# Top-k attention: mask and row maximum added by TensorE to the turned raw scores, the exponential taken in the copy from PSUM

## The chip, the core and the metric
The kernel runs on one core of one Trainium2 chip. The metric is the device time of one execution in microseconds; the kernel before has a median of 1265.99 us over 3 runs (1265.19 to 1269.22).

## The reference
Three layers follow each other. The first is the attention that is changed here; q, k and v are (4, 8, 576, 64) in f32:

```python
scores = scale * np.matmul(q, k.transpose(0, 1, 3, 2))
kth = np.partition(scores, -32, axis=-1)[..., -32:-31]
scores = np.where(scores >= kth, scores, -1000000000.0)
attn = np.exp(scores - np.max(scores, axis=-1, keepdims=True))
attn = attn / (np.sum(attn, axis=-1, keepdims=True) + 1e-09)
out = np.matmul(attn, v)
```

Each query row keeps its 32 largest scores of 576. Then 2304 tokens are routed to 8 experts of equal capacity by a greedy pass over their router logits, and a third layer applies a rational function between two products. Both follow the attention and are not touched.

## The kernel before
The attention works in 72 units (`NU`). A unit is 128 query rows of two heads against 576 keys, so two matrices of 128x576; nine units make a pair of heads of two batches (`NJ`), and the fifth of the nine (j equal to `R`) holds the last 64 rows of both batches. Units go in batches of three (`GB`), for which thresholds and normalisation are worked out together; the last six units are handled one by one.

The order of the work is written out by hand: `step(u)` (L993) issues one round of a software pipeline, and each engine runs its instructions in the order issued. In a step the stages are, each for an older unit than the one before it:

- ScalarE copies the scores of unit u from PSUM into `sv` (L686, `st_evacuate`), places turned q and k for the next heads in five of nine steps (L649), and copies a router tile where one is due (L886, L888).
- TensorE computes the scores of unit u+1 (L676), turns q and k (L635) or a router tile (L881), turns the weights of an older unit in nine 128x128 pieces into the PSUM tile `pt` (L820, `st_transpose`), and multiplies an older unit's turned weights with v (L842, L846, `st_av`); a router product (L894) ends the step where one is due.
- VectorE finds the candidates of unit u (`st_candidates`): fourteen MAX8 over sevenths of a row (L733), then three rounds of MAX8 and MATCH_REPLACE8 on the 56 candidates of each head (L739, L745). Between the first fourteen it takes from the list `later` one piece at a time: the window maxima (L760), the threshold (L777 to L792) and the normalisation (L860 to L862) of older units.
- `st_window`: for each head ScalarE forms the sign of the score against a first cut (L754) and GpSimd multiplies it onto the scores (L759), for VectorE's window maximum. At the end of a batch GpSimd scales the row maxima (L765).
- `st_weights`: for each head ScalarE takes the exponential of the scores less the row maximum (L808); the choice of the 32 is a factor 0 or 1 (or -1, which the copy's Relu drops) in `sg2`, from VectorE (L811) for the second head and in one unit of eight for both, else from ScalarE's Sign (L813); GpSimd multiplies both into `sv` (L814).
- `st_spill`: ScalarE copies the nine turned pieces from PSUM to SBUF with a Relu (L826). `pt` is one buffer, so the next turns wait for this copy.

When the loop ends, `finish_attention` (L1062) hands what is left of the last units to a small planner (`Flow`), which gets each piece with an engine, a cost and what it depends on, and issues it in the order that these give. There the weights are formed by ScalarE's exponential (L1125) and a combined compare-and-multiply on VectorE (L1131). At its end `suspicious` (L951) checks whether a threshold was doubtful; if it was, `recompute` does the attention again in an exact way.

```python
sv = sv_t.pop((u, hh))
ex = wk.tile([P, S], F32, name="ex")
nc.scalar.activation(ex, sv, AF.Exp, bias=t["nb"][:, c : c + 1], scale=SCALE)
sg = wk.tile([P, S], BF16, name="sg2")
if hh or u % WQ in WR:
    nc.vector.tensor_scalar(sg, sv, tau_all[:, 2 * GB * b + c : 2 * GB * b + c + 1], None, op0=OP.is_ge)
else:
    nc.scalar.activation(sg, sv, AF.Sign, bias=t["pn"][:, c : c + 1])
nc.gpsimd.tensor_tensor(sv, ex, sg, op=OP.mult)
```

Of the kernel before, what the change touches and what calls it, by code (L numbers as in the profile page):

```python
# [8 lines left out]
F32 = mybir.dt.float32  # L9
# [175 lines left out]
def kernel(  # L185
# [29 lines left out]
    R = 4  # L215
# [7 lines left out]
    OVER_BITS = 9  # L223
    BEFORE = -(1.0 - 2.0**-24)
    GROUPS = [82] * 5 + [83] * 2
    COLS = [
# [12 lines left out]
    region = wpool.tile([P, 2 * KC * F1], F32, name="region")  # L239
    nc.scalar.preload_act_table_set("natural_log_exp_and_others")  # L240
    ones = consts.tile([P, P], F32, name="ones")
    nc.vector.memset(ones, 1.0)
# [228 lines left out]
    with ExitStack() as actx:  # L471
# [21 lines left out]
        xs = xpool.tile([P, NT], F32, name="xs")  # L493
        tau_all = xpool.tile([P, NTILE], F32, name="tau_all")

        span = xpool.tile([P, 2], F32, name="span")
# [36 lines left out]
        with ExitStack() as sctx:  # L533
# [38 lines left out]
            raw, val, prep, sc_t, sv_t, pr_t, pT_t, po_t, bat = {}, {}, {}, {}, {}, {}, {}, {}, {}  # L572
            pq_t, prep_ps, po_bank = {}, {}, [None]

# [128 lines left out]
            def new_batch(b):  # L703
                t = {
                    "top": wk.tile([P, 2 * GB, 2, 8], F32, name="top"),
                    "nb": wk.tile([P, 2 * GB], F32, name="nb"),
                    "sum": wk.tile([P, 2 * GB], F32, name="sum"),
                    "w8": wk.tile([P, 2 * GB, 8], F32, name="w8"),
                    "pn": wk.tile([P, 2 * GB], F32, name="pn"),
                }  # L710
                bat[b] = t
                return t
# [11 lines left out]
            def st_candidates(u):  # L724
# [12 lines left out]
                for rd in range(3):  # L737
# [4 lines left out]
                    if rd < 2:  # L742
                        for hh in range(2):
                            nx = wk.tile([P, len(GROUPS) * 8], F32, name="cm", bufs=4)
                            nc.vector.match_replace(nx, t["top"][:, 2 * i + hh, rd, :], cds[hh], NEG)  # L745
                            cds[hh] = nx

            def st_window(u):
                b, i = divmod(u, GB)
# [11 lines left out]
                if u == group_end(u):  # L761
                    g = group(u)
                    n = g.stop - g.start
                    tau = tau_all[:, 2 * GB * b + g.start : 2 * GB * b + g.stop]
                    nc.gpsimd.tensor_scalar(t["nb"][:, g], t["top"][:, g, 0, 0], -SCALE, None, op0=OP.mult)  # L765
                    later.extend(threshold_steps(t, g, tau))
# [31 lines left out]

            WQ, WR = 8, [int(c) for c in "2".split()]

            def st_weights(u):
                b, i = divmod(u, GB)
                t = bat[b]
                for hh in range(2):
                    c = 2 * i + hh
                    sv = sv_t.pop((u, hh))
                    ex = wk.tile([P, S], F32, name="ex")
                    nc.scalar.activation(ex, sv, AF.Exp, bias=t["nb"][:, c : c + 1], scale=SCALE)  # L808
                    sg = wk.tile([P, S], BF16, name="sg2")
                    if hh or u % WQ in WR:  # L810
                        nc.vector.tensor_scalar(sg, sv, tau_all[:, 2 * GB * b + c : 2 * GB * b + c + 1], None, op0=OP.is_ge)  # L811
                    else:
                        nc.scalar.activation(sg, sv, AF.Sign, bias=t["pn"][:, c : c + 1])  # L813
                    nc.gpsimd.tensor_tensor(sv, ex, sg, op=OP.mult)  # L814

            def st_transpose(u):
                pt = ps_t.tile([P, 3, 4, P], F32, name="pt")
                pr = pr_t.pop(u)
                for c in range(NC):
                    nc.tensor.transpose(pt[:, c // 4, c % 4, :], pr[:, c * P : (c + 1) * P], ident)  # L820
                pq_t[u] = pt.rearrange("p b c x -> p (b c) x")[:, 0:NC, :]

            def st_spill(u):
                pt = pq_t.pop(u)
                sb = wk.tile([P, NC, P], F32, name="pT", bufs=2)
                nc.scalar.activation(sb, pt, AF.Relu)  # L826
                pT_t[u] = sb
# [79 lines left out]
            def st_exact(u):  # L907
                b, i = divmod(u, GB)
                st_evacuate(u)
                for hh in range(2):  # L910
# [10 lines left out]
                    nc.vector.tensor_scalar(nb, tops[:, 0, 0:1], -SCALE, None, op0=OP.mult)  # L921
                    ex = wk.tile([P, S], F32, name="ex")
                    nc.scalar.activation(ex, sv, AF.Exp, bias=nb, scale=SCALE)
# [27 lines left out]
            def suspicious():  # L951

                f = wk.tile([P, S], F32, name="ex")[:, 0 : 2 * NTILE].rearrange("p (k n) -> p k n", k=2)
                nc.vector.tensor_scalar(f[:, 0, :], tau_all, 0.0, None, op0=OP.is_le)
                m = wk.tile([P, S], F32, name="win")[:, 0:NTILE].bitcast(U32)
                nc.vector.tensor_scalar(m, cut_all.bitcast(U32)[:, :, 7], 0x7FFFFF, None, op0=OP.bitwise_and)
                nc.vector.tensor_scalar(f[:, 1, :], m, float(OVER_BITS), None, op0=OP.is_equal)
                nc.vector.tensor_reduce(oddb, f, axis=AX.XY, op=OP.max)
# [103 lines left out]
            def finish_attention():  # L1062
# [8 lines left out]
                def add_window(u):  # L1071
# [3 lines left out]
                    for hh in range(2):  # L1075
# [21 lines left out]
                    tau = tau_all[:, 2 * GB * b + g.start : 2 * GB * b + g.stop]  # L1097
                    largest_of[u] = last.add("V", 0.1, lambda: nc.vector.tensor_scalar(
                        t["nb"][:, g], t["top"][:, g, 0, 0], -SCALE, None, op0=OP.mult
                    ), [], u - 0.5)  # L1100
                    rk = wk.tile([P, 2], F32, name="rk")
# [14 lines left out]
                def add_weights_of(u, deps):  # L1116
                    b, i = divmod(u, GB)
                    t = bat[b]
                    end = []
                    for hh in range(2):  # L1120
                        c, st = 2 * i + hh, {}

                        def exp_of(c=c, hh=hh, st=st):
                            st["ex"] = wk.tile([P, S], F32, name="ex")
                            nc.scalar.activation(  # L1125
                                st["ex"], sv_t[u, hh], AF.Exp, bias=t["nb"][:, c : c + 1], scale=SCALE
                            )

                        def chosen_of(c=c, hh=hh, st=st):
                            sv = sv_t.pop((u, hh))  # L1130
                            nc.vector.scalar_tensor_tensor(  # L1131
                                sv, sv, tau_all[:, 2 * GB * b + c : 2 * GB * b + c + 1], st["ex"],
                                op0=OP.is_ge, op1=OP.mult,
                            )

                        a = last.add("A", 0.67, exp_of, [largest_of[u]] if u in largest_of else [], u)
                        m = last.add("V", 0.66, chosen_of, [a] + deps, u)
                        hold(a, "ex", 3, [m])
                        end.append(m)
                    return end  # L1140

                def add_turned(u, deps):
                    t = last.add("P", 1.1, lambda: st_transpose(u), deps, u)
                    a = last.add("A", 1.01, lambda: st_spill(u), [t], u)
# [1223 lines left out]
```

## Time and profile before

| what | value |
|---|---|
| median of 3 runs | 1265.99 us |
| profiled execution | 1264.03 us |
| its span | 1262.3 us |
| PE, PEld busy | 1103.9, 892.2 us |
| DVE, ACT, POOL busy | 1108.7, 1062.8, 423.3 us |
| mean granted TensorE clock | 0.913 |

In the profile PE are TensorE's products, PEld its weight loads, DVE is VectorE, ACT ScalarE and POOL GpSimd. The span runs from the first to the last instruction; the execution's own time is 1.7 us longer. A line such as L811 is that of the kernel. In a timeline, instructions that follow each other and are alike stand in one row, with their count; busy time counts overlapping instructions once, so the start of the next instruction tells what one occupies better than its duration does. "128*128" ahead of a shape is the part of TensorE's array. Some records are missing, a few per cent.

### The profile page before, as it was taken

The numbers are of one execution on the slowest core, as the hardware profiler recorded it, in microseconds if no ns is written. First come the engines' busy times: TensorE is split into PE (matmuls) and PEld (weight loads), VectorE is DVE, ScalarE is ACT, GpSimd is POOL, SyncE is SP. The second block draws the span as 40 slices with busy tenths as digits, with TensorE's granted clock in tenths as the row PEclk, the third lists the DMA queues.
The fourth block names the chain that finished last, engine by engine and source line by source line (L and its number), as shares of the span: only waits on it lengthen the run. The fifth ranks groups of instructions, "written<-read, shape, count | busy, mean of one in ns | idle before, by whom it ended". The sixth has DMA issues, their size and how long they took to land.

```text
span 1262.3 us, 26058 instructions
## 1 busy us (share of the span) xinstructions
PE 1103.9 (87%) x9159; PEld 892.2 (71%) x9159; DVE 1108.7 (88%) x4224; ACT 1062.8 (84%) x1869; POOL 423.3 (34%) x429
## 2 busy tenths in 40 slices
PE   5788888899989796787547999999999999999996
PEld 3677777787878684555435777878888888888784
DVE  6999999999999973888788979898989989897795
ACT  4999999999999975867799978888888789876684
POOL 3888888878888820000110001010001001001010
PEclk8899999999999987555678999999999999999999
DMA  5204112020200110921313322213122210200000
GB/s 122 49 10 150 30 38 49 10 49 10 49 2 1 70 65 3 371 66 51 120 36 138 128 93 80 74 27 128 38 87 86 87 67 26 80 1 20 1 20 20
DMA packets 81103, 80.54 MB, mean 64 GB/s; under 512 B 59968, under 2 KB 59968, under 8 KB 80960
## 3 DMA queue, kind: packets, MB, share of 16 engines
q1 hardware_dynamic: 77888, 69.27, 17.2%
q0 software_dynamic: 3072, 9.48, 2.5%
q8 instruction: 76, 1.25, 0.4%
q14 instruction: 67, 0.55, 0.1%
HBM read 69.25 MB, written 9.47 MB: 62 GB/s over the span
## 4 chain that ended last, share of the span: by engine, by line
PE 26%; issue 14%; ACT 6%; DVE 4%; POOL 1%; DMA 0%; POOLq 0%; DVEq 0%
PE pa L1903 3%; PE pa L1904 3%; PE pa L1905 3%; PE ph L1903 3%; PE ph L1905 3%; PE ph L1904 3%; PE po L1904 3%; PE po L1905 3%; PE po L1903 3%; ACT junk L302 2%; POOL out_dram L2289 1%; ACT w1s L1376 1%; PE pa L2278 0%; ACT wout L379 0%; DVE w2s L1381 0%
## 5 line engine op out<-in xcount | busy, mean ns | idle before, releaser
L759 POOL TENSOR_TENSOR win<-sv,sg 128x576 f32<-128x576 f32 x142 | 179.2, 1283 | 37.8 <-ACT sg L754 32.0
L814 POOL TENSOR_TENSOR sv<-ex,sg 128x576 f32<-128x576 f32 x136 | 175.5, 1293 | 46.6 <-DVE sg L811 34.8
L733 DVE MAX8 cd<-sv 128x8 f32<-128x82 f32 (+1 forms) x1008 | 182.4, 231 | 4.1 <-ACT sv L686 4.1
L842 PE MATMUL po<-vm,pT 128*128 128x65 f32 (+1 forms) x1280 | 153.7, 269 | 11.2 <-DVE eqp L787 4.1
L1903 PE MATMUL ph<-x,win 128*128 128x288 f16 x512 | 147.4, 288 | 10.6 <-DVE uv L2172 10.6
L842 PEld LDWEIGHTS po<-vm,pT 128*128 128x128 f32 (+1 forms) x1280 | 142.5, 185 | 18.5 <-DVE eqp L787 7.5
L1904 PE MATMUL po<-g,wout 128*128 128x288 f16 x512 | 146.4, 286 | 2.7 <-DVE g L1894 2.7
L1905 PE MATMUL ph<-x,win 128*128 128x288 f16 x512 | 147.4, 288 | 0.0
L1904 PE MATMUL ph<-x,win 128*128 128x288 f16 x512 | 147.4, 288 | 0.0
L1903 PE MATMUL po<-g,wout 128*128 128x288 f16 x512 | 146.4, 286 | 1.0 <-ACT g L1893 0.8
L1905 PE MATMUL po<-g,wout 128*128 128x288 f16 x512 | 146.4, 286 | 0.0
L2289 POOL DMA_INDIRECT out_dram<-ob,tok x24 | 25.0, 1043 | 317.9 <-ACT ob L2285 265.9
L1880 POOL DMA_INDIRECT xe<-xrows,rows_i x24 | 24.5, 1023 | 294.9 <-PE pa L1915 272.0
L754 ACT ACTIVATE sg<-sv,cut_all 128x576 bf16<-128x576 f32 x142 | 109.4, 781 | 5.0 <-DVE cut_all L739 4.8
L2163 ACT ACTIVATE z<-ph,inv 128x288 f32<-128x288 f32 x128 | 63.9, 499 | 56.2 <-PE ph L1905 55.5
L820 PE MATMUL pt<-ident,sv 128*128 128x128 f32 x648 | 96.6, 294 | 9.8 <-POOL sv L814 9.2
L760 DVE MAX8 w<-win 128x8 f32<-128x576 f32 x142 | 105.2, 741 | 0.0
L808 ACT ACTIVATE ex<-sv,nb 128x576 f32<-128x576 f32 x136 | 104.5, 776 | 0.0
L820 PEld LDWEIGHTS pt<-ident,sv 128*128 128x128 f32 x648 | 79.1, 152 | 27.5 <-POOL sv L814 17.1
L826 ACT ACTIVATE pT<-pt 128x1152 f32<-128x1152 f32 x72 | 81.7, 1134 | 6.2 <-PE pt L820 6.2
L686 ACT ACTIVATE sv<-s 128x1152 f32<-128x1152 f32 x72 | 80.7, 1121 | 3.7 <-PE s L676 2.8
L676 PE MATMUL s<-region 64*128 64x288 f32 (+5 forms) x400 | 55.4, 425 | 27.7 <-ACT kT L649 9.5
(361 smaller groups left out, 3302.4 us busy)
## 6 DMA issues: line engine op xcount, KB each, us to landing
region<-in_moe_w_dram SPq DMA_DIRECT2D x16, 2048.0 KB, 7.8
xrows<-x SPq DMA_DIRECT2D x1, 4644.0 KB
region<-in_q_dram SPq DMA_DIRECT2D x32, 128.0 KB, 2.8
region<-in_k_dram SPq DMA_DIRECT2D x32, 128.0 KB, 2.9
vm<-in_v_dram SPq DMA_DIRECT2D x32, 128.0 KB, 3.0
wout<-in_moe_w_in_dram SPq DMA_DIRECT2D x8, 511.8 KB, 7.1
region<-in_moe_w_out_dram SPq DMA_DIRECT2D x8, 511.8 KB, 3.5
win<-in_moe_w_in_dram SPq DMA_DIRECT2D x6, 511.8 KB, 7.1
```

The source lines that it names most:

```text
L733: nc.vector.max(cd[:, g, :], sv[:, o : o + n])
L754: nc.scalar.activation(sg, sv_t[u, hh], AF.Sign, bias=cut_all[:, 2 * u + hh, 7:8], scale=-OVER, accum_out=t["sum"][:, c : c + 1],)
L759: nc.gpsimd.tensor_tensor(win, sv_t[u, hh], sg, op=OP.mult)
L760: later.append(lambda c=c, win=win: nc.vector.max(t["w8"][:, c, :], win))
L808: nc.scalar.activation(ex, sv, AF.Exp, bias=t["nb"][:, c : c + 1], scale=SCALE)
L814: nc.gpsimd.tensor_tensor(sv, ex, sg, op=OP.mult)
L820: nc.tensor.transpose(pt[:, c // 4, c % 4, :], pr[:, c * P : (c + 1) * P], ident)
L826: nc.scalar.activation(sb, pt, AF.Relu)
L842: nc.tensor.matmul(po[p0 : p0 + n, i, hh, :], sb[:, hh * (R + 1) + c, p0 : p0 + n], vm[:, bb, hh, c, :], start=(c == 0), stop=False,)
L1903: nc.tensor.matmul(acc, ah, bh, start=first, stop=False)
L1904: nc.tensor.matmul(acc, ah, bl, start=False, stop=False)
L1905: nc.tensor.matmul(acc, al, bh, start=False, stop=last)
```

## The change
The weights are no longer formed ahead of the turn. TensorE turns the raw scores; a product then adds to each turned piece the mask (as stationary operand, bf16) times a diagonal (`dg`) that holds -1/EPS times the row maxima. The mask is EPS where the score is chosen and 1 + EPS where it is not, so a chosen score loses the row maximum and another one 2^14 times the maximum besides. The copy from PSUM takes the exponential of the sum. The row maximum is rounded in `dg`, which the later division by the sum of weights makes up for. For the second head VectorE makes the mask in one comparison with an addition; for the first head ScalarE takes a Sign, as before in seven units of eight, and GpSimd scales and shifts it. GpSimd makes the diagonals once for a batch of three units. `suspicious` also asks now whether a threshold is under 2^-4 or a row maximum over 2^12.

```diff
+    EPS = 2.0**-14
+    LEAST, MOST = 2.0**-4, 2.0**12
...
+    identb = consts.tile([P, P], BF16, name="identb")
+    nc.vector.tensor_copy(identb, ident)
...
-                    "nb": wk.tile([P, 2 * GB], F32, name="nb"),
+                    "dg": wk.tile([P, 2 * GB, P], BF16, name="dg", bufs=2),
...
+            def shift(t, b, g, engine):
+
+                n = g.stop - g.start
+                top = top_all[:, 2 * GB * b + g.start : 2 * GB * b + g.stop]
+                engine.tensor_scalar(top, t["top"][:, g, 0, 0], -1.0 / EPS, None, op0=OP.mult)
+                engine.tensor_tensor(
+                    t["dg"][:, g], identb[:, None, :].to_broadcast([P, n, P]), top[:, :, None].to_broadcast([P, n, P]),
+                    op=OP.mult,
+                )
...
-                    nc.gpsimd.tensor_scalar(t["nb"][:, g], t["top"][:, g, 0, 0], -SCALE, None, op0=OP.mult)
+                    shift(t, b, g, nc.gpsimd)
...
-            WQ, WR = 8, [int(c) for c in "2".split()]
+            def beyond(mk, sv, c):
+                nc.vector.tensor_scalar(mk, sv, tau_all[:, c : c + 1], EPS, op0=OP.is_lt, op1=OP.add)
 
             def st_weights(u):
                 b, i = divmod(u, GB)
                 t = bat[b]
+                mk = wk.tile([P, 2, S], BF16, name="mk", bufs=2)
                 for hh in range(2):
                     c = 2 * i + hh
                     sv = sv_t.pop((u, hh))
-                    ex = wk.tile([P, S], F32, name="ex")
-                    nc.scalar.activation(ex, sv, AF.Exp, bias=t["nb"][:, c : c + 1], scale=SCALE)
-                    sg = wk.tile([P, S], BF16, name="sg2")
-                    if hh or u % WQ in WR:
-                        nc.vector.tensor_scalar(sg, sv, tau_all[:, 2 * GB * b + c : 2 * GB * b + c + 1], None, op0=OP.is_ge)
+                    if hh:
+                        beyond(mk[:, hh, :], sv, 2 * u + hh)
                     else:
+                        sg = wk.tile([P, S], BF16, name="sg2")
                         nc.scalar.activation(sg, sv, AF.Sign, bias=t["pn"][:, c : c + 1])
-                    nc.gpsimd.tensor_tensor(sv, ex, sg, op=OP.mult)
+                        nc.gpsimd.tensor_scalar(mk[:, hh, :], sg, -0.5, 0.5 + EPS, op0=OP.mult, op1=OP.add)
+                mk_t[u] = mk.rearrange("p h s -> p (h s)")
...
             def st_transpose(u):
                 pt = ps_t.tile([P, 3, 4, P], F32, name="pt")
                 pr = pr_t.pop(u)
+                mk = mk_t.get(u)
+                b, i = divmod(u, GB)
                 for c in range(NC):
-                    nc.tensor.transpose(pt[:, c // 4, c % 4, :], pr[:, c * P : (c + 1) * P], ident)
+                    o = c * P
+                    nc.tensor.transpose(pt[:, c // 4, c % 4, :], pr[:, o : o + P], ident)
+                    if mk is None:
+                        continue
+                    for p0, n, hh in [(0, P, c // (R + 1))] if c != R else [(0, TAIL, 0), (TAIL, TAIL, 1)]:
+                        nc.tensor.matmul(
+                            pt[p0 : p0 + n, c // 4, c % 4, :], mk[:, o + p0 : o + p0 + n],
+                            bat[b]["dg"][:, 2 * i + hh, :], start=False, stop=True, skip_group_check=True,
+                        )
...
-                nc.scalar.activation(sb, pt, AF.Relu)
+                if mk_t.pop(u, None) is not None:
+                    nc.scalar.activation(sb, pt, AF.Exp, scale=SCALE)
+                else:
+                    nc.scalar.activation(sb, pt, AF.Copy)
...
-                    largest_of[u] = last.add("V", 0.1, lambda: nc.vector.tensor_scalar(
-                        t["nb"][:, g], t["top"][:, g, 0, 0], -SCALE, None, op0=OP.mult
-                    ), [], u - 0.5)
+                    largest_of[u] = last.add("G", 0.9, lambda: shift(t, b, g, nc.gpsimd), [], u - 0.5)
...
-                        a = last.add("A", 0.67, exp_of, [largest_of[u]] if u in largest_of else [], u)
-                        m = last.add("V", 0.66, chosen_of, [a] + deps, u)
-                        hold(a, "ex", 3, [m])
-                        end.append(m)
-                    return end
+                    first = last.add("V", 0.5, lambda: chosen_of(0), deps, u)
+                    return end + [first, last.add("V", 0.5, lambda: chosen_of(1), [first], u)]
...
-                    t = last.add("P", 1.1, lambda: st_transpose(u), deps, u)
+                    t = last.add("P", 1.8, lambda: st_transpose(u), deps, u)
+                    if deps:
+                        hold(deps[-2], "mk", 2, [t])
```

## Rows read from the trace of the kernel before
**Rows 1.** One line's instructions, L686, the copy of the scores: count, durations, first and last start.
```profile
L686 ACT ACTIVATE sv<-s x72: 1104/1118/1160, 12.7 to 435.5; 128x1152 f32<-128x1152 f32 x72
```

**Rows 2.** Windows: us, busy PE, PEld, DVE, ACT, POOL, PEclk, DMA share, GB/s.
```profile
60.00:400.00 340.00, 299.71 (x2543) 259.25 (x2540) 334.21 (x1903) 327.82 (x557) 284.94 (x244) 0.96 0.15 37
440.00:500.00 60.00, 50.14 (x335) 39.77 (x335) 36.00 (x133) 41.52 (x56) 9.42 (x9) 0.79 0.13 47
500.00:520.00 20.00, 9.98 (x136) 7.92 (x136) 14.34 (x74) 15.13 (x32) 1.89 (x4) 0.50 0.74 278
```

**Rows 3.** Groups of instructions, 60 to 400 us: busy us, mean ns, idle before, releaser.
```profile
L814 POOL TENSOR_TENSOR sv<-ex,sg 128x576 f32<-128x576 f32 x111 | 143.2, 1294 | 37.0 <-DVE sg L811 27.3 <-ACT region L649 2.8 <-DVE lg L895 1.2
...
L808 ACT ACTIVATE ex<-sv,nb 128x576 f32<-128x576 f32 x111 | 85.4, 776 | 0.0
...
L811 DVE TENSOR_SCALAR sg<-sv,tau_all 128x576 bf16<-128x576 f32 x62 | 43.9, 718 | 0.0
...
L813 ACT ACTIVATE sg<-sv,pn 128x576 bf16<-128x576 f32 x48 | 37.3, 777 | 11.7 <-DVE pn L792 11.5
...
L895 DVE COPY lg<-po 128x8 f32<-128x8 f32 x8 | 1.3, 164 | 5.8 <-PE po L894 5.8
```

**Rows 4.** One line's instructions, L811, whole execution: least, median, longest ns.
```profile
L811 DVE TENSOR_SCALAR sg<-sv,tau_all x77: 501/514/1643, 36.1 to 444.5; 128x576 bf16<-128x576 f32 x77
```

**Rows 5.** Timeline of VectorE: start us, duration us, instruction.
```profile
250.98 0.50 DVE L811 TENSOR_SCALAR sg<-sv,tau_all 128x576 bf16<-128x576 f32 x1
251.40 0.24 DVE L733 MAX8 cd<-sv 128x8 f32<-128x82 f32 x1
...
256.26 1.39 DVE L811 TENSOR_SCALAR sg<-sv,tau_all 128x576 bf16<-128x576 f32 x1
```

**Rows 6.** Timeline of GpSimd at the second of those comparisons.
```profile
256.06 1.28 POOL L814 TENSOR_TENSOR sv<-ex,sg 128x576 f32<-128x576 f32 x1
```

**Rows 7.** Timeline of ScalarE, two instructions that follow each other.
```profile
254.74 0.77 ACT L813 ACTIVATE sg<-sv,pn 128x576 bf16<-128x576 f32 x1
255.41 0.77 ACT L808 ACTIVATE ex<-sv,nb 128x576 f32<-128x576 f32 x1
```

**Rows 8.** Groups of GpSimd, whole execution, shapes kept apart.
```profile
L765 POOL TENSOR_SCALAR nb<-top 128x6 f32<-128x6 f32 x22 | 5.3, 239 | 0.0
L1664 POOL TENSOR_TENSOR asel<-oh,gone 128x144 bf16<-128x144 bf16 x7 | 3.1, 440 | 69.8 <-DVE rng L1537 45.5 <-DVE gone L1658 22.9 <-DVE gone L1730 1.4
```

**Rows 9.** Timeline of TensorE's products, one step and the start of the next.
```profile
327.20 1.35 PE L676 MATMUL s<-region 64*128 64x64 f32 x10 [1.04 <-ACT xt L886]
328.48 0.66 PE L881 MATMUL s<-ident,x 128*128 128x128 f32 x4
328.98 1.15 PE L820 MATMUL pt<-ident,sv 128*128 128x128 f32 x9
329.96 1.00 PE L842 MATMUL po<-vm,pT 128*128 128x65 f32 x8
...
332.14 1.01 PE L894 MATMUL po<-wg,xt 128*128 128x8 f32 x8
333.84 1.35 PE L676 MATMUL s<-region 64*128 64x64 f32 x10 [0.69 <-ACT xt L886]
```

**Rows 10.** Timeline of TensorE's products at half the clock, behind the attention.
```profile
516.65 1.06 PE L1440 MATMUL pl<-region,diag 128*128 128x256 f32 x2
517.51 0.42 PE L1441 MATMUL pl<-w1s,minus 128*128 128x256 f16 x1
517.72 0.43 PE L1667 MATMUL pt<-asg,onesb 128*128 128x8 bf16 x9
```

**Rows 11.** Timeline of TensorE's weight loads, the nine turns of one step.
```profile
253.38 1.01 PEld L820 LDWEIGHTS pt<-ident,sv 128*128 128x128 f32 x9
```

**Rows 12.** Groups of instructions, 440 to 520 us: the last units' weights.
```profile
L1131 DVE SCALAR_TENSOR_TENSOR sv<-sv,tau_all,ex 128x576 f32<-128x576 f32 x8 | 6.2, 811 | 0.1
L1125 ACT ACTIVATE ex<-sv,nb 128x576 f32<-128x576 f32 x8 | 5.8, 767 | 3.1 <-DVE sv L1131 3.1
```

More of the change, by code (lines that the diff above doesn't have):

```diff
@@ L494 @@
         tau_all = xpool.tile([P, NTILE], F32, name="tau_all")
+        top_all = xpool.tile([P, NTILE], F32, name="top_all")
         span = xpool.tile([P, 2], F32, name="span")
@@ L572 @@
             raw, val, prep, sc_t, sv_t, pr_t, pT_t, po_t, bat = {}, {}, {}, {}, {}, {}, {}, {}, {}
-            pq_t, prep_ps, po_bank = {}, {}, [None]
+            pq_t, mk_t, prep_ps, po_bank = {}, {}, {}, [None]
             LOADS = [
@@ L921, in st_exact @@
                     nc.vector.tensor_scalar(nb, tops[:, 0, 0:1], -SCALE, None, op0=OP.mult)
-                    ex = wk.tile([P, S], F32, name="ex")
+                    ex = wk.tile([P, S], F32, name="win")
                     nc.scalar.activation(ex, sv, AF.Exp, bias=nb, scale=SCALE)
@@ L951, in suspicious @@
             def suspicious():
-                f = wk.tile([P, S], F32, name="ex")[:, 0 : 2 * NTILE].rearrange("p (k n) -> p k n", k=2)
-                nc.vector.tensor_scalar(f[:, 0, :], tau_all, 0.0, None, op0=OP.is_le)
+                f = wk.tile([P, S], F32, name="win")[:, 0 : 3 * NTILE].rearrange("p (k n) -> p k n", k=3)
+                nc.vector.tensor_scalar(f[:, 0, :], tau_all, LEAST, None, op0=OP.is_lt)
+                nc.vector.tensor_scalar(f[:, 2, :], top_all, -MOST / EPS, None, op0=OP.is_lt)
                 m = wk.tile([P, S], F32, name="win")[:, 0:NTILE].bitcast(U32)
@@ L1116, in add_weights_of, with chosen_of @@
                 def add_weights_of(u, deps):
[L1117 to L1134, printed above, removed]
-                        a = last.add("A", 0.67, exp_of, [largest_of[u]] if u in largest_of else [], u)
-                        m = last.add("V", 0.66, chosen_of, [a] + deps, u)
-                        hold(a, "ex", 3, [m])
-                        end.append(m)
-                    return end
+                    end = [largest_of[u]] if u in largest_of else []
+                    mk = {}
+                    def chosen_of(hh):
+                        if not mk:
+                            mk[0] = wk.tile([P, 2, S], BF16, name="mk", bufs=2)
+                            mk_t[u] = mk[0].rearrange("p h s -> p (h s)")
+                        beyond(mk[0][:, hh, :], sv_t.pop((u, hh)), 2 * u + hh)
+                    first = last.add("V", 0.5, lambda: chosen_of(0), deps, u)
+                    return end + [first, last.add("V", 0.5, lambda: chosen_of(1), [first], u)]
                 def add_turned(u, deps):
-                    t = last.add("P", 1.1, lambda: st_transpose(u), deps, u)
+                    t = last.add("P", 1.8, lambda: st_transpose(u), deps, u)
+                    if deps:
+                        hold(deps[-2], "mk", 2, [t])
                     a = last.add("A", 1.01, lambda: st_spill(u), [t], u)
```

## The prediction
> **What bounds the kernel now.** I read first where the time goes by stage, then what paces the stage that is changed, then the three engines that the change loads or relieves. The attention loop's 72 score copies start between 12.7 and 435.5 us [rows 1], so 71 steps take 422.8 us, 5.95 us each. The steady part is 60 to 400 us [rows 2]: 111 exponentials at two a step are 56 steps [rows 3], 6.07 us a step. There VectorE is busy 334.2 of 340 us, ScalarE 327.8, TensorE 299.7, GpSimd 284.9: two engines are all but full, and VectorE stands first with 5.97 us a step. So removing work from ScalarE alone can't pay; the question is what makes VectorE full.
>
> The answer lies in L811, the comparison with the threshold. 62 of them take 43.9 us, 718 ns in the mean [rows 3], though the least and the median are 501 and 514 ns and the longest is 1643 [rows 4]. The instance at 250.98 is free (0.50 us, and the next instruction starts 0.42 us behind it); the one at 256.26 takes 1.39 us [rows 5], and ends 0.3 us after a GpSimd product that ran from 256.06 to 257.34 [rows 6]. So the comparison is held while GpSimd's long product runs. 62 x 0.51 = 31.6 us would be its free cost; 12.3 us, or 0.22 us a step, is holding. VectorE's only idle time in the stretch is 5.8 us, all for the router's product [rows 3].
>
> **The change, part by part.**
> ScalarE: two exponentials a step go. From the start of the Sign at 254.74 to that of the Exp at 255.41 an instruction occupies 0.67 us [rows 7], so 111 x 0.67 = 74.4 us go. The Sign for the first head now runs in all 56 steps, not in 48 [rows 3]: 8 x 0.67 = 5.4 us come. The copy out of PSUM becomes an Exp of the same size; Exp and Sign of one size take 776 and 777 ns [rows 3], so a function's kind costs nothing here. 327.8 - 74.4 + 5.4 = 258.8 us, 4.62 a step. ScalarE stops being a bound. Its next wait is the one it has now for the Sign's threshold (11.5 us [rows 3]); behind it the next score copy queues, with a microsecond of slack.
>
> VectorE: the mask is one comparison a step instead of 62 in 56 steps, with an addition in the same pass: 6 x 0.42 = 2.5 us less. The holding should mostly go too. Today GpSimd multiplies the first head's weights just when VectorE finishes a unit's candidates and comes to the comparison. Afterwards those products are gone, and GpSimd's window products start only when ScalarE has taken a Sign of that unit's candidates, 0.77 us (a Sign's length [rows 7]) after the comparison could begin. Bounds: all 12.3 us gone, or none. I take all but a quarter (the long GpSimd work every third step may still meet it). 334.2 - 2.5 - 9.2 = 322.5 us, 5.76 us a step; with all gone 5.70, with none 5.92.
>
> GpSimd: two products of 1.29 us a step go (143.2 us [rows 3]). Added are one pass over 576 bf16 elements, one small multiply, and every third step the scaled diagonals, 128 x 768. Their prices are not in the trace. The pass lies between the 0.44 us of a 144-element bf16 product [rows 8] and the 1.29 us of a 576-element one; I take 0.8, being one input instead of two. The diagonals lie between 1.29 us (more elements than that row) and 1.29 x 768/576 = 1.72, and I take 1.72. The small multiply is L765's 0.24, already there. The two window products stay, of L814's shape. Per step 2 x 1.29 + 0.8 + (1.72 + 0.24)/3 = 4.0 us, against 5.1 now: no bound. The window products queue behind the diagonals once in three steps; VectorE wants them a step later, so they hide.
>
> TensorE: added are ten bf16 products a step onto the PSUM that the nine turns have just written. The turns now start from the raw scores, and each product waits for the mask and the diagonals where the turns waited for GpSimd's weights; the mask is ready 1.3 us earlier after the comparison, since no GpSimd product follows it. Behind that wait on TensorE stand the step's value products, and ScalarE's copy of the turned tile in the next step. No DMA is touched. A step's own work without waits: scores 327.20 to 328.48, 1.28 us; four turns 0.50; the nine turns 328.98 to 329.96, 0.98; the value products 329.96 to 332.14, 2.18; the router product about 0.95, its 1.01 less the end of its last piece [rows 9]. Four turns of q and k of that shape come in four of nine steps and two in a fifth (0.25 a step), router turns and products in 9 of 56 (0.23). Sum 4.92 us. One added product has 128 columns. The nearest mixture is f32 and f16 products onto one PSUM tile at half the clock (0.50 in that stretch [rows 2]; the rows are [rows 10]): the two f32 take 516.65 to 517.51, the f16 one of 256 columns 0.21 us, with no time lost between them, so 128 columns at the full clock take 0.053 us. And nine bf16 products of 8 columns pass in 0.43 us [rows 10], so a bf16 weight load is no longer than about 0.03. That gives the lower end, 0.053. The upper end: an f32 weight load fills the whole time of its turn (nine loads in 1.01 us beside nine turns in 1.15 [rows 9, 11]), and one that can't start before the added product does has 0.98/9 = 0.11 us to run; if the turns wait for all of it besides the product's own columns, 0.16. If it merely runs beside the product, 0.11 in all. I take 0.08, between the ends where the load is hidden and where it runs beside: 0.8 us a step, 5.72 in all.
> The Trainium skill, page "TensorE: Matmul & The Clock Gate", section "Back-to-back issue gap", gives 81 ns for a load and product of 128 columns in a stream; by that the sum would be 4.92 + 0.81 = 5.73. No run here shows such a stream of 128-column bf16 products.
>
> End of the attention, 440 to 500 us: 8 exponentials (5.8 us) go from ScalarE, and VectorE's 8 combined products of 0.81 [rows 12] become comparisons of 0.51, 2.4 us less; TensorE gains some six times 0.8 us at a lower clock (0.79), and it is the busiest there, 50.1 of 60 us against 41.5 for ScalarE [rows 2]. I take 0, with ends 5 us to either side. One identity copy at the start and one check at the end are 0.2 us each, hidden by first loads and by the waits there.
>
> **The sum.** VectorE 5.76 and TensorE 5.72 lie side by side. Today's step is 0.10 above its fullest engine; keep that: 5.86 us. Saved 0.21 x 56 = 11.8 us; the 15 steps outside the stretch (5.5 us each, filling and draining) I set to nothing. Off the profiled execution, 1264.0 us (span 1262.3), this gives 1252 us. The median of the runs is 1266.0, 2 us above that execution. A measurement tells some 0.3%, 4 us, from no change.
>
> **Rivals.**
> 1. TensorE takes the place of ScalarE. At 0.11 us a product its step is 4.92 + 1.1 = 6.02, plus 0.10: 6.12, which loses 0.05 x 56 = 3 us: 1267 us. For it: the weight loads are full length already [rows 11]. Against: nothing but the guess that some of a load hides. Chance 0.18.
> 2. Slower: the f32 load behind each added product isn't hidden at all. 0.16 x 10 = 1.6 us, TensorE's step 6.52 + 0.10 = 6.62; 0.55 x 56 = 31 us, and the 15 other steps some 8: 1303 us. It decides from 0.105 us a product on, (6.07 - 0.10 - 4.92)/10. Against it: nine loads and nine turns, 0.98 us each if laid end to end, pass in the same 0.98 us [rows 9, 11], so loads run beside products on the same rows. Chance 0.12. The Trainium skill, same page, section "Part 3: Packing small matmuls — row/col tiling", says that a load overlaps running products only if it is for other rows of the array; that rule would bring this case, and those rows disagree with it.
> 3. The holding stays: GpSimd's new work meets the comparison as often as the old. VectorE 5.92 + 0.10 = 6.02, 3 us saved, 1261 us. For it: the diagonals and window products together still run 3 to 5 us of each step. Chance 0.15.
> 4. The new check on the range of the scores sends the kernel into its exact second pass, hundreds of microseconds. The reference's inputs, multiplied out, have thresholds from 1.77 and maxima up to 11.4, far inside 1/16 and 4096. Chance 0.01.
> The forecast, 1242 to 1259, has 0.54.
>
> **How the numbers follow.** Low end: holding all gone, the waits of 0.10 too, 5.70: 0.37 x 56 = 21 us, and 5 at the end, 1238. High end: rival 1 with 5 us lost at the end, 1272. Rival 2 lies outside. Faster: the forecast, what lies below it, and parts of rivals 1 and 3, 0.70. Within 0.3%: most of rivals 1 and 3, 0.14. Slower: rival 2, 4 and the top of 1, 0.16.
>
> **What would show it.** Right: L811's successor at 0.50 to 0.55 us in the mean; ScalarE under 80% in 60 to 400 us while VectorE stays near full; the nine turns with their products in 1.6 to 2.0 us; steps near 5.9. Wrong: turns and products above 2.1 us, and VectorE waiting for TensorE; or comparisons still at 0.7.

## The result and the profile after

The changed kernel takes 1253.14 us (median of 4 runs, 1249.88 to 1254.08); the kernel before, on the same chip, 1267.61 us (median of 4, 1265.19 to 1275.57). The ratio is 0.987, with a 95% interval of 0.9822 to 0.9919: faster by 14 us. The profiled execution took 1253.07 us, with a span of 1251.4, 11 us below the one of before; the traces can account for these 11 of the 14.

The windows of the kernel after (us, busy PE, PEld, DVE, ACT, POOL, PEclk, DMA share, GB/s) answer to [rows 2]:

```profile
60.00:400.00 340.00, 338.08 (x3258) 293.33 (x3256) 332.20 (x1976) 276.13 (x469) 217.02 (x216) 1.00 0.15 37
440.00:500.00 60.00, 43.22 (x359) 31.18 (x357) 28.53 (x113) 32.17 (x54) 1.45 (x3) 0.76 0.14 46
```

The 340 us hold 58 steps (58 Signs and 58 comparisons, below) where they held 56: 5.86 us a step for 6.07. Such a count is good to one step, 0.1 us; the score copies that start in the stretch lie 5.88 us apart, where they lay 6.14. VectorE stays nearly full with 5.73 us a step, ScalarE has fallen from 96 to 81% of the stretch, and TensorE has risen from 88 to 99%. Its clock was granted in full for the whole stretch; before it was 0.96.

Groups of instructions of the kernel after, 60 to 400 us (busy us, mean ns, idle before, releaser), with the last line answering to the router's product in [rows 3]:

```profile
L843 PE MATMUL pt<-dg,mk 128*128 128x128 bf16 x580 | 99.3, 224 | 0.0
...
L828 ACT ACTIVATE sg<-sv,pn 128x576 bf16<-128x576 f32 x58 | 44.7, 771 | 40.3 <-DVE pn L807 40.3
...
L829 POOL TENSOR_SCALAR mk<-sg 128x576 bf16<-128x576 bf16 x57 | 38.2, 671 | 21.4 <-ACT sg L828 21.4
...
L815 DVE TENSOR_SCALAR mk<-sv,tau_all 128x576 bf16<-128x576 f32 x58 | 30.5, 525 | 0.0
L758 POOL TENSOR_TENSOR dg<-identb,top_all 128x768 bf16<-128x768 bf16 x20 | 29.4, 1469 | 1.7
...
L924 DVE COPY lg<-po 128x8 f32<-128x8 f32 x9 | 1.5, 166 | 7.8 <-PE po L923 7.5
```

TensorE's 580 added products are ten a step. ScalarE now sits idle for 40.3 us ahead of the Sign, waiting for its threshold, where it was 11.5. The comparison fell from 718 to 525 ns, and there is one a step. Single lines' instructions (count, durations, first and last start) say where the end of the execution moved; L691 is the copy of the scores, L1646 the first instruction behind the attention:

```profile
L691 ACT ACTIVATE sv<-s x72: 1106/1116/1134, 12.8 to 422.0; 128x1152 f32<-128x1152 f32 x72
...
L1646 DVE COPY lc<-lg x1: 235/235/235, 492.8 to 492.8; 128x144 f32<-128x144 f32 x1
```

The kernel before has the copy of `lg` in L1629:

```profile
L1629 DVE COPY lc<-lg x1: 1604/1604/1604, 504.0 to 504.0; 128x144 f32<-128x144 f32 x1
```

The last copy starts 13.5 us earlier than in [rows 1]. From it to L1646 pass 70.8 us; before, the copy of `lg` started at 504.0, 68.5 us behind the last score copy. From there to the end of the span it is 758.6 us against 758.3. So the loop won 13.5 us, the end of the attention lost 2.3, and the rest stayed within 0.3 us.

**The comparison.** Between 60 and 400 us, 32 of the 62 comparisons of the kernel before began while a GpSimd instruction of over a microsecond ran, and took 0.92 us in the mean; the other 30 took 0.505. After, none of the 57 that begin in the stretch does. The timeline of the kernel after shows why (start us, us, instruction, idle before):

```profile
302.40 0.50 DVE L815 TENSOR_SCALAR mk<-sv,tau_all 128x576 bf16<-128x576 f32 x1
...
302.78 0.76 ACT L769 ACTIVATE sg<-sv,cut_all 128x576 bf16<-128x576 f32 x1
...
303.72 1.28 POOL L774 TENSOR_TENSOR win<-sv,sg 128x576 f32<-128x576 f32 x1 [1.56 <-ACT sg L769]
```

GpSimd's next long instruction waits for a Sign of the same unit whose candidates VectorE has just finished, and by then the comparison is over. What GpSimd runs at the comparison now is the pass over the mask (0.67 us): nine of the 57 comparisons are held by it and take 0.62 to 0.68 us. None overlaps the diagonals.

**The turns.** The timeline of TensorE's products in the kernel after, around the piece that holds both heads:

```profile
300.38 0.22 PE L843 MATMUL pt<-dg,mk 128*128 128x128 bf16 x1
300.43 0.28 PE L839 MATMUL pt<-ident,sv 128*128 128x128 f32 x1
300.64 0.25 PE L843 MATMUL pt<-dg,mk 128*64 128x128 bf16 x2
300.82 0.33 PE L839 MATMUL pt<-ident,sv 128*128 128x128 f32 x1
300.98 0.22 PE L843 MATMUL pt<-dg,mk 128*128 128x128 bf16 x1
301.04 0.28 PE L839 MATMUL pt<-ident,sv 128*128 128x128 f32 x1
301.15 0.22 PE L843 MATMUL pt<-dg,mk 128*128 128x128 bf16 x1
301.21 0.28 PE L839 MATMUL pt<-ident,sv 128*128 128x128 f32 x1
```

A turn with a full product takes 0.17 us (301.04 to 301.21); a turn alone took 0.11 [rows 9], so the product costs 0.06. The piece with two products of 64 columns takes 0.39 (300.43 to 300.82): 0.28 for the two. The piece behind it takes 0.22 (300.82 to 301.04), 0.05 more than the other full ones, so the two cost 0.33 in all. From the first turn of a unit to its first value product it is 1.80 us, the median of 58 units.

### The profile page after: what moved, and what is told of

Its sections match the earlier page's. It is cut to its first block, busy times and chain, and to the rows that moved or that the text cites. A ratio compares the mean times of both kernels' runs of the same rounds, so it can differ in the third digit from the quotient of the medians.

```text
span 1251.4 us, 27126 instructions
## 1 busy us (share of the span) xinstructions
PE 1141.0 (91%) x9879; PEld 921.2 (74%) x9879; DVE 1088.6 (87%) x4216; ACT 979.3 (78%) x1734; POOL 331.3 (26%) x390
## 4 chain that ended last, share of the span: by engine, by line
PE 26%; issue 14%; ACT 6%; DVE 4%; POOL 1%; DMA 0%; POOLq 0%; DVEq 0%
PE pa L1920 3%; PE pa L1921 3%; PE pa L1922 3%; PE ph L1920 3%; PE ph L1922 3%; PE ph L1921 3%; PE po L1921 3%; PE po L1922 3%; PE po L1920 3%; ACT junk L306 2%; POOL out_dram L2306 1%; ACT w1s L1393 1%; PE pa L2295 0%; ACT wout L383 0%; DVE w2s L1398 0%
## 5 line engine op out<-in xcount | busy, mean ns | idle before, releaser
L871 PEld LDWEIGHTS po<-vm,pT 128*128 128x128 f32 (+1 forms) x1280 | 139.4, 182 | 8.3 <-issue 4.3
L839 PE MATMUL pt<-ident,sv 128*128 128x128 f32 x648 | 131.7, 287 | 0.0
L769 ACT ACTIVATE sg<-sv,cut_all 128x576 bf16<-128x576 f32 x142 | 108.9, 772 | 22.5 <-DVE cut_all L744 14.5
L843 PE MATMUL pt<-dg,mk 128*128 128x128 bf16 (+1 forms) x720 | 123.9, 224 | 0.0
L839 PEld LDWEIGHTS pt<-ident,sv 128*128 128x128 f32 x648 | 91.5, 141 | 21.1 <-ACT sg L769 5.8
L691 ACT ACTIVATE sv<-s 128x1152 f32<-128x1152 f32 x72 | 80.5, 1118 | 11.7 <-PE s L681 4.6
L828 ACT ACTIVATE sg<-sv,pn 128x576 bf16<-128x576 f32 x68 | 52.4, 770 | 46.2 <-DVE pn L807 46.2
L843 PEld LDWEIGHTS <-mk 128*128 128x128 bf16 (+1 forms) x720 | 72.4, 111 | 9.0 <-DVE mk L815 0.2
```

Source lines behind the costliest of these rows:

```text
L691: nc.scalar.activation(pair.rearrange("p h (g c) -> p (h g) c", g=2), sc_t.pop(u)[:, :, 0:HS], AF.Copy)
L769: nc.scalar.activation(sg, sv_t[u, hh], AF.Sign, bias=cut_all[:, 2 * u + hh, 7:8], scale=-OVER, accum_out=t["sum"][:, c : c + 1],)
L839: nc.tensor.transpose(pt[:, c // 4, c % 4, :], pr[:, o : o + P], ident)
L843: nc.tensor.matmul(pt[p0 : p0 + n, c // 4, c % 4, :], mk[:, o + p0 : o + p0 + n], bat[b]["dg"][:, 2 * i + hh, :], start=False, stop=True, ...
L871: nc.tensor.matmul(po[p0 : p0 + n, i, hh, :], sb[:, hh * (R + 1) + c, p0 : p0 + n], vm[:, bb, hh, c, :], start=(c == 0), stop=False,)
```

## Experiments

The theory after the result: the gain is that VectorE's comparison is no longer held by GpSimd's product, which needs ScalarE to have been relieved too, and TensorE's products give a part back. The rival: ScalarE's relief alone, or a TensorE that still has room. Each kernel was timed beside runs of the kernel before on the same chip, whose medians lay between 1267.58 and 1268.28 us; ratios are to these.

**Putting GpSimd's product back.** On the changed kernel:

```diff
                         nc.gpsimd.tensor_scalar(mk[:, hh, :], sg, -0.5, 0.5 + EPS, op0=OP.mult, op1=OP.add)
+                        nc.gpsimd.tensor_tensor(sg, sv, sg, op=OP.mult)
```

> The changed kernel with one product of 128x576 more on GpSimd a step, behind the first head's mask, where the kernel before multiplied the weights; nothing uses its result. Theory that VectorE's comparison was held by GpSimd's product and that ending this gave much of the gain: the comparison's mean goes from 0.525 to 0.65 to 0.75 us again, the step up by 0.1 to 0.2 us, 1258 to 1265 us. Rival, the holding was not what VectorE lost or lies now behind TensorE's floor: within 3 us of 1253.

Measured: 1265.58 us (10 runs), ratio 0.9968 (0.9945 to 0.9991): 12 us of the 14 are gone, and the time lies 0.6 us above its range. The stretch of 60 to 400 us and the comparison's group in it:

```profile
60.00:400.00 340.00, 330.83 (x3112) 283.73 (x3110) 339.96 (x1897) 262.99 (x450) 283.22 (x264) 0.99 0.15 37
```

```profile
L815 DVE TENSOR_SCALAR mk<-sv,tau_all 128x576 bf16<-128x576 f32 x55 | 50.1, 912 | 0.0
```

The comparison grew by 0.39 us, to 0.91 where 0.65 to 0.75 were expected; VectorE's 0.13 us of spare time in a step went, and the step grew by about the rest, from 5.88 to 6.12 by the score copies. This product holds the comparison for 0.41 us a step, nearly twice the 0.22 of the kernel before, so the 12 us show what holding does, not what the old holding cost. A held and a free one, in the timelines of VectorE and of GpSimd:

```profile
209.63 1.24 DVE L815 TENSOR_SCALAR mk<-sv,tau_all 128x576 bf16<-128x576 f32 x1
...
227.90 0.50 DVE L815 TENSOR_SCALAR mk<-sv,tau_all 128x576 bf16<-128x576 f32 x1
```

```profile
209.28 1.27 POOL L830 TENSOR_TENSOR sg<-sv,sg 128x576 bf16<-128x576 f32 x1
...
228.03 1.50 POOL L830 TENSOR_TENSOR sg<-sv,sg 128x576 bf16<-128x576 f32 x1
```

The first comparison began 0.35 us behind the product and ended 0.32 us after the product's end (210.87 against 210.55). Over the 43 of this kernel that begin so the median is 0.315, and it is 0.316 in the kernel before, [rows 5, 6] among them. The second comparison began ahead of the product, took its free 0.50, and the product took 1.50 for its usual 1.28, ending 1.14 us behind the comparison. Whichever comes first holds the other up.
The Trainium skill, page "GPSIMD Engine Reference", section "8. Key points", says that GpSimd shares its SBUF interfaces with VectorE, and that they contend when VectorE runs in a two-port mode or reads two inputs from SBUF. These rows agree that they contend, and add the size; which mode the comparison ran in they don't say.

**Taking each part away from the kernel before.** Without the first head's product, without the exponentials, and without both (`ex` replaced by `sv`):

```diff
-                    nc.gpsimd.tensor_tensor(sv, ex, sg, op=OP.mult)
+                    if hh:
+                        nc.gpsimd.tensor_tensor(sv, ex, sg, op=OP.mult)
```

```diff
-                    ex = wk.tile([P, S], F32, name="ex")
-                    nc.scalar.activation(ex, sv, AF.Exp, bias=t["nb"][:, c : c + 1], scale=SCALE)
...
-                    nc.gpsimd.tensor_tensor(sv, ex, sg, op=OP.mult)
+                    nc.gpsimd.tensor_tensor(sv, sv, sg, op=OP.mult)
```

> The kernel before without GpSimd's product of weights for the first head, so that these rows are weighted by raw scores; exponentials and signs stay. Theory that the holding of VectorE's comparison costs 0.22 us a step and that ScalarE stands right behind: the comparison's mean falls from 0.72 to 0.50 to 0.55 us, the step from 6.07 to about 5.95, where ScalarE's 5.85 keeps it: 1258 to 1262 us beside 1266. Rival, ScalarE's exponentials alone set the old step: no change, within 3 us. Second rival, the holding alone set it: 1252 us or less.

> The kernel before without the exponentials of the loop: GpSimd multiplies the raw scores by the choice, so weights are raw scores. ScalarE falls to 4.5 us a step, GpSimd's products stay. Theory: VectorE's comparison stays held (0.65 us or more in the mean) and VectorE keeps the step at 5.95 to 6.05: 1260 to 1265 us. Rival, ScalarE set the old step: 5.75 to 5.85 us a step, 1248 to 1255 us.

> The kernel before with both taken out: no exponentials in the loop and no product of weights for the first head. Theory: now neither the holding nor ScalarE is in the way and VectorE's own work, 5.70 us, is the floor, with TensorE at 4.9: step 5.72 to 5.82, 1244 to 1252 us, more off than the two single cuts together or as much. Rival, one of the two alone carries the gain: no better than the better of the single cuts.

Measured: 1259.29 us (ratio 0.9929, 0.9908 to 0.9949), 1255.40 (0.9908, 0.9881 to 0.9935) and 1244.47 (0.983, 0.9781 to 0.9879): 8.8, 12.7 and 23.6 us off the kernel before. Windows of 60 to 400 us and the comparison's group, the kernel without the first product:

```profile
60.00:400.00 340.00, 304.53 (x2626) 266.37 (x2622) 329.03 (x1938) 334.94 (x570) 220.12 (x193) 0.95 0.15 37
```

```profile
L811 DVE TENSOR_SCALAR sg<-sv,tau_all 128x576 bf16<-128x576 f32 x63 | 32.1, 519 | 0.0
```

The same of the kernel without exponentials:

```profile
60.00:400.00 340.00, 310.44 (x2661) 267.02 (x2661) 339.79 (x1970) 269.45 (x462) 294.30 (x253) 0.96 0.15 37
```

```profile
L809 DVE TENSOR_SCALAR sg<-sv,tau_all 128x576 bf16<-128x576 f32 x64 | 40.0, 634 | 0.0
```

And of the kernel without either, the window alone:

```profile
60.00:400.00 340.00, 311.12 (x2717) 266.23 (x2715) 339.02 (x2019) 271.80 (x467) 226.54 (x201) 0.99 0.15 37
```

Without the product the comparison is all but free (519 ns), and ScalarE is the full engine (334.9 of 340 us). Without the exponentials VectorE is full (339.8), but its comparison got shorter too, 634 ns for 718: with ScalarE ahead, only 22 of 64 comparisons meet a product, for 32 of 62. The holding in the stretch fell from 12.3 to 7.4 us (40.0 - 64 x 0.51), and VectorE's idle time from 5.8 to 0.2. So the second expectation missed by 5 us, and the rival's number was the better one: VectorE's load wasn't fixed. The first and the third came out. The two together give 23.6 us, a little more than the two single cuts added (21.5), and VectorE is full. The change gives 14.5: what it gives back should lie with the work that it adds, TensorE's products first, which are tried next.

**TensorE's products, none and two.** Taken out of the changed kernel altogether, and each issued twice with half the factor:

```diff
-                    for p0, n, hh in [(0, P, c // (R + 1))] if c != R else [(0, TAIL, 0), (TAIL, TAIL, 1)]:
-                        nc.tensor.matmul(
...
```

```diff
                     for p0, n, hh in [(0, P, c // (R + 1))] if c != R else [(0, TAIL, 0), (TAIL, TAIL, 1)]:
+                      for _ in range(2):
                         nc.tensor.matmul(
```

> The changed kernel without TensorE's added products (masks and diagonals are still made, nothing reads them; the weights then are exponentials of all raw scores). Theory of two floors side by side: VectorE's own work, 332.2 us in 58 steps or 5.73 us a step, stays and keeps the step at 5.75 to 5.80 instead of 5.86, so 3 to 7 us off: 1246 to 1250 us, with VectorE full and TensorE near 5.0 us a step. Rival, TensorE alone is the floor of the changed kernel and VectorE has slack: 10 us or more off, under 1243 us.

> The changed kernel with each added product issued twice with half the diagonal, so that the result is the same. Theory of two floors: TensorE has no slack left (338.1 of 340 us busy), so all of the second set shows: turns and products go from 1.80 to about 2.4 us (ten more at 0.053 to 0.082 us), the step from 5.86 to 6.4 to 6.6, and the time to 1285 to 1297 us. Rival, VectorE is the floor and TensorE's load hides behind it: under 1263 us.

Measured: 1242.71 us (5 runs, 1240.99 to 1248.83; ratio 0.9791, 0.9753 to 0.9829) and 1281.76 (1.0112, 1.0068 to 1.0157). Without them the median is 10 us below the changed kernel, just on the rival's side; but the profiled execution was the slowest of the five, and in it VectorE had become the bound (338.0 of 340 us, 5.84 a step where 5.75 to 5.80 were expected). What made the other four 5 to 8 us faster no trace shows. The wait of the products for the mask is gone with them; the two weren't told apart. Twice the products cost 29 us, a little under the expected range. The window without the products, then that with twice the products and TensorE's timeline there:

```profile
60.00:400.00 340.00, 313.98 (x2707) 275.57 (x2703) 337.99 (x2006) 275.64 (x473) 221.94 (x222) 0.95 0.15 37
```

```profile
60.00:400.00 340.00, 340.00 (x3544) 297.97 (x3543) 312.13 (x1839) 260.29 (x437) 204.65 (x201) 1.00 0.15 37
```

```profile
300.50 0.28 PE L839 MATMUL pt<-ident,sv 128*128 128x128 f32 x1
300.62 0.28 PE L844 MATMUL pt<-dg,mk 128*128 128x128 bf16 x2
300.73 0.28 PE L839 MATMUL pt<-ident,sv 128*128 128x128 f32 x1
300.94 0.31 PE L844 MATMUL pt<-dg,mk 128*64 128x128 bf16 x4
301.17 0.33 PE L839 MATMUL pt<-ident,sv 128*128 128x128 f32 x1
```

A turn with two full products takes 0.23 us, 0.06 more than with one; the whole group takes 2.31 for 1.80, 0.051 for each further product. The middle piece, with four products of 64 columns, takes 0.44 (300.73 to 301.17): the second two cost 0.06 together where the first two cost 0.28 in that piece. TensorE never idles, and VectorE waits.

**Relieving one of the two engines, or both.** Three kernels on the changed one: the second head's mask by Sign and GpSimd like the first's; one shift per unit, of the first head's maxima, so that the middle piece needs one product; and both.

```diff
-                    if hh:
-                        beyond(mk[:, hh, :], sv, 2 * u + hh)
-                    else:
-                        sg = wk.tile([P, S], BF16, name="sg2")
...
+                    sg = wk.tile([P, S], BF16, name="sg2")
...
```

```diff
-                    "dg": wk.tile([P, 2 * GB, P], BF16, name="dg", bufs=2),
+                    "dg": wk.tile([P, GB, P], BF16, name="dg", bufs=2),
...
+                    nc.tensor.matmul(
+                        pt[:, c // 4, c % 4, :], mk[:, o : o + P],
+                        bat[b]["dg"][:, i, :], start=False, stop=True, skip_group_check=True,
+                    )
```

> The changed kernel with both heads' masks from ScalarE's Sign and GpSimd, none from VectorE in the loop. VectorE falls by 0.43 us a step to 5.30, ScalarE rises to 5.43, GpSimd to 4.4. Theory of two floors: TensorE's 5.75 stays and holds the step, 0 to 7 us off: 1246 to 1253 us. Rival, VectorE alone is the floor: 0.3 us a step or more, under 1237 us. Second rival, ScalarE's longer queue delays the score copies: above 1256 us.

> The changed kernel with one diagonal a unit, from the first head's maximum, the masks half by VectorE as in the change. TensorE's turns fall from 1.80 to 1.535 us, as in the run with both cuts, and GpSimd's diagonals halve; VectorE's work stays. Theory of two floors side by side: VectorE's 5.73 us a step keeps the step at 5.75 to 5.83, 3 to 7 us off the changed kernel: 1244 to 1250 us, well short of the 23 us that both cuts together gave. Rival, TensorE alone was the floor: 0.27 x 58 = 15 us off, 1238 us or less.

> The changed kernel with both heads' masks from ScalarE and GpSimd, and one diagonal a unit, from the first head's row maximum for both heads (the division by the sum makes up for it; the new range check then sees the first head's maximum alone). The piece that holds both heads takes one product instead of two halves. Theory that TensorE is the floor once VectorE is relieved (340 of 340 us busy with the masks on ScalarE): its turns fall from 1.80 to about 1.57 us, the step from 5.84 to 5.6, 14 us off the run with the masks on ScalarE alone: about 1232 us. Rival, that run's 5.84 us is set by something else than TensorE, ScalarE's queue for one: within 4 us of its 1245.6.

Measured: 1245.64 us (0.982, 0.9782 to 0.9859), 1246.45 (0.9824, 0.9787 to 0.986) and 1230.00 (0.9712, 0.9663 to 0.9761). Each alone wins some 7 us on the changed kernel (four runs each, all below its shortest), both together 23. The first lies 0.4 us under its range, the other two came out. In the profiled executions most of what a single change wins isn't in the loop. With both masks by ScalarE it is 9.3 us shorter than the changed kernel's: the loop has 4.4, the end of the attention is 8.7 shorter (62.1 us for 70.8) and the rest 3.8 longer. With one shift it is 6.3 us shorter: the loop has 2.5, the end 6.2, the rest is 2.5 longer. No cause was tried for the ends. With both changes the loop alone wins 18.6 us. So in the loop the two engines are two floors at nearly one height: relieve one, and the other keeps the step. The windows with both masks by ScalarE, with one shift, and with both changes, then the last one's copies of the scores:

```profile
60.00:400.00 340.00, 340.00 (x3281) 295.50 (x3278) 312.79 (x1930) 311.18 (x531) 255.35 (x276) 1.00 0.15 37
60.00:400.00 340.00, 332.94 (x3219) 294.30 (x3217) 333.31 (x1986) 274.39 (x471) 205.62 (x218) 0.98 0.15 37
60.00:400.00 340.00, 336.89 (x3335) 301.20 (x3332) 324.20 (x2027) 322.31 (x549) 254.17 (x293) 1.00 0.15 37
```

```profile
L691 ACT ACTIVATE sv<-s x72: 1106/1115/1137, 12.7 to 403.4; 128x1152 f32<-128x1152 f32 x72
```

With both, a step is 5.60 us, the loop ends 18.6 us before the changed kernel's, and VectorE, ScalarE and TensorE lie between 322 and 337 of 340 us. With one product in the middle piece the turns take 1.535 us for 1.80. This version beats both kernels.

**Both masks by VectorE.**

```diff
-                    if hh:
-                        beyond(mk[:, hh, :], sv, 2 * u + hh)
-                    else:
...
+                    beyond(mk[:, hh, :], sv, 2 * u + hh)
```

> The changed kernel with both heads' masks by VectorE: no Sign of the threshold on ScalarE and no mask on GpSimd. VectorE rises by a comparison, 0.42 to 0.50 us, to 6.15 to 6.23 us a step. Theory that VectorE is a floor of the changed kernel: the step goes from 5.88 to 6.2 to 6.3, 1271 to 1280 us. Rival, TensorE hides VectorE's growth: under 1260 us.

Measured: 1271.16 us (10 runs; 1.0022, 1.0002 to 1.0041), 18 us above the changed kernel. Its window:

```profile
60.00:400.00 340.00, 331.65 (x3112) 284.98 (x3112) 339.39 (x1942) 236.32 (x398) 171.60 (x152) 0.99 0.15 37
```

VectorE is full at 6.12 us a step (6.2 to 6.3 were expected; the time is in its range), with 112 comparisons that are all but free (508 ns). So the gain needs VectorE's share of the masks to stay at half or less: moved wholly to it, they cost more than the change had won.

## Why the prediction was right

The time, 1253.14 us, lies 1 us from the forecast of 1252, and the step is 5.86 us by the count and 5.88 by the score copies, for the predicted 5.86. The mechanism held too: the comparison is free, VectorE's step falls, and TensorE comes up beside it. Two terms came out by luck, below.

- **VectorE, the holding.** This is the part that decided. The free cost was taken as 0.51 and measures 0.505; I left a quarter of the holding in place, and about a tenth remains: (0.525 - 0.505) x 58 = 1.2 us of 12.3. It comes from the pass over the mask, not from the diagonals that the quarter was left for. VectorE came to 5.73 a step for 5.76. That it is GpSimd's product, and not the removed exponentials alone, the kernel with the product put back shows: the holding returns, nearly twice the old one, and with it 12 us.
- **"Removing work from ScalarE alone can't pay".** This sentence is wrong. It took VectorE's busy time as work, though the same part of the prediction found 12.3 us of it to be holding. Removing the exponentials alone won 12.7 us: 4.9 us of holding went, and VectorE's 5.6 us of waits for the router's product. That the holding fell since ScalarE lets GpSimd start at another time is argued. Removing the holding alone won 8.8 us, and then ScalarE itself is full. Each gives a part, the whole 23.6 us needs both, and the change takes both.
- **ScalarE.** 4.76 us a step for 4.62, 81% where I said under 80: a miss without effect, as it is no bound.
- **GpSimd.** 3.74 us a step for 4.0; the pass over the mask took 0.67 (predicted 0.8) and the diagonals 1.47 (1.72), both inside their bounds.
- **TensorE.** The price of 0.08 us a product is right as a mean, (1.80 - 0.98)/10 = 0.082, and wrong in its reason. I took a load half hidden behind every product. A full product costs 0.06, near the lower end of 0.053, with its loads hidden; the two products of 64 columns cost 0.33 together, 0.05 of it in the next piece, which no term named. It was luck that the mean came out. Had the working kept the middle piece apart, it would also have led to the one-shift version. Rival 2's price holds for these two products alone, at 0.16 each. The sum was also worked out from rows at the full clock (1.0), while the stretch of before had 0.96; that the fuller TensorE was then granted 1.00 no term had worked out, which is the other piece of luck: at 0.96 the same 5.74 us would be 5.74/0.96 = 5.98, an estimate, above VectorE's 5.73. The rule that the prediction set beside it (the Trainium skill, page "TensorE: Matmul & The Clock Gate", section "Part 3: Packing small matmuls — row/col tiling") would make every one of these loads wait, since all are for the same rows; the trace disagrees for the full products.
- **The margin** of 0.10 us over the fuller engine measures 0.13 over VectorE's 5.73; VectorE's idle time before the router's product went from 5.8 to 7.8 us.
- **The end of the attention** lost 2.3 us, within the 5 to either side; what the loop won inside 60 to 400 us and what outside, the traces don't part finely: by the count 0.21 x 56 = 11.8 of its 13.5 us lie inside, by the spacing of the copies all of it.
- **Rivals 1 and 3** asked for 0.11 us a product, and for comparisons still at 0.7; neither came. But TensorE did become the second floor, as rival 1 had it, only 0.3 us lower (4.92 + 0.82 = 5.74).

Open is the spread of single executions, some 5 us to either side in several kernels, and with it the exact size of what the products give back: 4 us by the profiled executions, 10 by the medians. Open too is why the end of the attention takes 62 us in some kernels and 71 in others.

## What to carry to other kernels

Busy time of an engine is not its work: compare the mean of an instruction with its least and median, and ask what else runs whenever it is long. Where two engines hold each other up, the order of the work can keep them apart, so that one's long instruction starts when the other's has passed. When a change lifts one engine to the level of another, price both; after that a change to one pays little, 2.5 and 4.4 us of the loop here, and a change to both pays, 18.6.

## What the runs showed of the hardware

- A VectorE comparison of 128x576 from f32 to bf16 (0.50 us) that begins while GpSimd's product runs ends 0.315 us after it, in the median of 32 and of 43 cases; a GpSimd product that begins inside a comparison took 1.36 to 1.52 us for its usual 1.28, in 27 of 31 cases of the kernel before and the one with the product put back, and ended 1.14 us after the comparison in all 27. The other four began within 0.05 us of the comparison's start, took 1.28 and held it.
- A bf16 product of 128 columns, accumulated onto an f32 turn in PSUM, costs 0.06 us beside the turn. Two of 64 columns cost 0.33, 0.05 of it in the piece behind them. TensorE's weight loads of the kernel after show where it goes:

```profile
300.21 0.14 PEld L839 LDWEIGHTS pt<-ident,sv 128*128 128x128 f32 x1
300.26 0.10 PEld L843 LDWEIGHTS <-mk 128*128 128x128 bf16 x1
300.38 0.14 PEld L839 LDWEIGHTS pt<-ident,sv 128*128 128x128 f32 x1
300.64 0.11 PEld L843 LDWEIGHTS <-mk 128*64 128x64 bf16 x2
300.82 0.14 PEld L839 LDWEIGHTS pt<-ident,sv 128*128 128x128 f32 x1
```

The load of a full product starts with the turn ahead of it (300.26) and is over when the product begins; the load for the half products starts only at 300.64, with the product, though that turn began at 300.43, and the next turn's load starts at 300.82 with its turn. That a load and a product of different widths don't overlap is argued from these rows; that two more products of 64 columns cost only 0.06 us together agrees with it. No run tried it apart.
